# Where the MLP turns the next block's tokens: from between the two second layers of a step to the middle of its first layer

## The chip, the cores and the metric

The kernel runs on one core of a Trainium2 chip. The metric is the device time of one execution in microseconds (us). TensorE (PE in the profile) multiplies, ScalarE (ACT), VectorE (DVE) and GpSimd (POOL) do elementwise work, SyncE (SP) issues transfers. PEld is TensorE's loading of weights, which overlaps the matmuls.

## The reference

The change lies in the last of three stages (an attention, a mixture of experts, an MLP):

```python
def _moe2_ref(x, w_in, w_out, a, b):          # x: 1792 x 768, w_in: 768 x 2048, w_out: 2048 x 768
    h = x @ w_in                              # first layer
    P = a[0] + a[1] * h + a[2] * h**2 + a[3] * h**3
    Q = 1.0 + np.abs(b[0]) * np.abs(h) + np.abs(b[1]) * h**2
    g = P / (Q + 1e-06)                       # the rational function
    return (g @ w_out).astype(np.float32)     # second layer
```

## The kernel before

The MLP starts near 600 us of the span. Its 1,792 tokens go in five blocks (`BLOCKS`): four of three tiles of 128 tokens and one of two. A block has 16 steps, one for each 128 of the 2,048 hidden features, so there are 80 steps, numbered n; f is the step's place in its block. Operands are split into a high and a low part, so every product is three matmuls.

The order on every engine is the order in which `blocks` writes the instructions; nothing reorders them. A step n issues:

- `first(n)` (L1348 to L1350): 18 matmuls, 6 pieces of the depth by 3, into one of the two PSUM banks of the ring `ph` (the tiles `p_l1`; the trace calls both `p_l`).
- `wout_high` (L1326, ScalarE) and, further down, `wout_low` (L1334, VectorE or GpSimd): the split of a row of w_out that is used two steps later. In the first block VectorE has the low part in even steps and GpSimd in odd ones.
- `win_load(n + 3)` (L1314): a transfer that GpSimd issues.
- `rational(n)`, first part: five ScalarE instructions (L1360 to L1364), of which the first four read the bank of `first(n)`; three on GpSimd (L1365 to L1367); the reciprocal on VectorE (L1368), which waits for the second GpSimd one (L1366).
- `second(0, n - 4)` (L1383 to L1385): nine matmuls (six in the last block). 
- In the steps f = 4, 6, ..., 14 of the blocks 0 to 3 a turn (`x2_pose`): three transposes on TensorE (L1306; two for the last block's tokens) of one sixth of the next block's tokens into a bank, the high part copied out by ScalarE (`pose(0)`, L804), the low part taken by VectorE (`pose(1)`, L806: bank minus high part).
- `rational(n - 1)`, third part: ScalarE's cast to gh (L1373), VectorE's gl (L1374). `rational(n)`, second part: VectorE's product t (L1370), which needs the reciprocal and gh's source.
- `second(1, n - 16)`: nine more matmuls, from the second block on. In the first block a step has 27 matmuls, later 36.

`turn` hands out the tiles of a ring in rotation. Before, a step with a turn takes two banks of `ph`: `first(n)` the one, the transposes the other, and `first(n + 1)` again the one, so that `first(n + 2)` gets the bank of the transposes.

So VectorE's order over a step with a turn is: reciprocal of n, gl of n - 1, product of n, `pose(1)`, `wout_low`. ScalarE's is: `wout_high`, five of `rational(n)`, `pose(0)`, gh of n - 1.

Of the kernel before, what the change touches and what calls it, by code (L numbers as in the profile page):

```python
# [40 lines left out]
class K:  # L41
# [1255 lines left out]
        with self.nc.allow_non_contiguous_dma("one column"):  # L1297
            self.nc.sync.dma_start(out=self.order, in_=self.x2d[1][:N, 384].rearrange("(t p) -> p t", p=128))

    def x2_pose(self, bi, kc, bank="ph"):  # L1300

        nc = self.nc
        nt = self.BLOCKS[bi][1]
        pt = self.turn(bank)[:, : 128 * nt]
        for t in range(nt):
            nc.tensor.transpose(pt[:, 128 * t : 128 * t + 128], self.xr[t // 2][:, t % 2, 128 * kc : 128 * kc + 128], self.ident)  # L1306
        h, l = (x[kc][:, : 128 * nt] for x in self.x2[bi % 2])
        return lambda part: self.split(h, l, pt, parts=(part,))
# [95 lines left out]
    def blocks(self):  # L1404
        NF, L, NB = self.NF, self.LAG, len(self.BLOCKS)
        rat, out = self.started, []
        total = NB * NF
        for n in range(total + NF):
            b, f = divmod(n, NF)
            second = [n - L, n - NF]  # L1410
            if b < NB:
                if n not in rat:
                    ph = self.first(n)
            for nh in range(2):
                self.wout_high(nh, second[nh] + 2)
            if n:
                self.win_load(n + 3)
            if b < NB:
                if n not in rat:
                    rat[n] = self.rational(ph, n)  # L1420
                    next(rat[n])
            pose = None
            if 0 <= second[0] < total:
                self.second(0, second[0])
            if b + 1 < NB and 4 <= f < 16 and f % 2 == 0:
                pose = self.x2_pose(b + 1, (f - 4) // 2)
                pose(0)
            if n - 1 in rat:
                next(rat[n - 1])
            if b < NB:  # L1430
                next(rat[n])
            if pose:
                pose(1)
            for nh in range(2):
                self.wout_low(nh, second[nh] + 2)
            if out:
                out.pop(0)()
            last = n >= total + NF - 2
            if 0 <= second[1] and not last:
                self.second(1, second[1])  # L1440
            for nh in range(2):
                if second[nh] >= 0 and second[nh] % NF == NF - 1 and not last:
                    bi = second[nh] // NF
                    if bi < NB:
                        out += [self.result(bi, nh, t) for t in range(self.BLOCKS[bi][1])]
            if f == 0 and b + 1 < NB:
                self.x2_load(self.BLOCKS[b + 1])
            if n == 4:
                self.targets()
            if n == NF - 7:  # L1450
                for k in range(3):
                    self.wout_load(1, k)
        for x in out:
            x()

        nt = self.BLOCKS[-1][1]
        for t in range(nt):
            self.second(1, total - 2, [t])
            self.second(1, total - 1, [t])
            self.result(NB - 1, 1, t, t == nt - 1)()  # L1460
# [31 lines left out]
```

## Time and profile before

| | |
|---|---|
| median of 3 runs | 1111.56 us (1111.51 to 1115.95) |
| profiled execution: its own time | 1112.95 us |
| profiled execution: span | 1111.3 us |
| share of the span busy: PE, PEld, DVE, ACT, POOL | 95%, 77%, 62%, 60%, 63% |
| mean granted TensorE clock | 0.981 of full speed |

The shares are means over three stages with different limits, so the argument goes by the MLP's own stretches. A line of the trace in order of time has the start, the duration, the engine, the line of the kernel, the operation with its output and inputs, and in brackets the engine's idle time before it and what ended it. Instructions of one engine overlap a little at their ends: a matmul of 384 columns shows 0.33 us, and the next starts 0.17 us after it.

### The profile page before, as it was taken

The page shows a single profiled execution, that of the slowest core. Times are in us where ns is not written, and L with a number is a line of the kernel's source. Part 1 is how long each engine was busy: PE and PEld are TensorE (multiplying, and loading weights), DVE is VectorE, ACT ScalarE, POOL GpSimd, SP SyncE. Part 2 cuts the span into 40 slices and gives each one's busy share as a digit, 9 for nine tenths or more (in the row PEclk, how much of TensorE's full clock was granted, in tenths as well). Part 3 has the DMA queues.
Part 4 walks back from the last instruction along what each step waited for, and adds up shares of the span by engine and source line. Part 5 has one row for each costly group of instructions (what it writes and reads, how often), then busy time and mean ns, then how long its engine had stood idle before and what let it go on. Part 6 is the DMA issues. An engine that isn't in the chain of part 4 may idle for free. (4 is left out here: it accounts for less than half of the span.)

```text
span 1111.3 us, 17228 instructions
## 1 busy us (share of the span) xinstructions
PE 1055.2 (95%) x5808; PEld 856.9 (77%) x5808; DVE 689.6 (62%) x862; ACT 672.3 (60%) x1052; POOL 701.6 (63%) x738
## 2 busy tenths in 40 slices
PE   6999999988999989998999889999999999999995
PEld 2332333247898989888889788999999999999995
DVE  3457575878558645936273877666666666665661
ACT  5777777762556535744353666666666666576662
POOL 5767676642546443635253777786787788779974
PEclk8999999998999999999999899999999999999999
DMA  7787878763889775968526565766576566557843
GB/s 190 231 260 227 261 224 262 261 224 133 305 308 366 255 273 166 364 226 305 166 73 225 171 211 167 252 195 196 179 247 216 184 219 214 194 191 232 259 153 112
DMA packets 96441, 247.12 MB, mean 222 GB/s; under 512 B 12321, under 2 KB 61377, under 8 KB 96321
## 3 DMA queue, kind: packets, MB, share of 16 engines
q1 hardware_dynamic: 78624, 161.22, 44.1%
q0 software_dynamic: 17248, 82.62, 22.7%
q10 hardware_dynamic: 448, 1.80, 0.4%
q8 instruction: 60, 0.98, 0.4%
q14 instruction: 61, 0.49, 0.1%
HBM read 202.93 MB, written 42.67 MB: 221 GB/s over the span
## 5 line engine op out<-in xcount | busy, mean ns | idle before, releaser
L1368 DVE RECIPROCAL raw<-raw 128x384 f32<-128x384 f32 (+1 forms) x80 | 191.4, 2392 | 160.6 <-POOL raw L1366 160.6
L840 PE MATMUL p_l<-w1h,x 128*128 128x512 f32 x432 | 143.9, 400 | 1.4 <-ACT x L804 1.4
L1365 POOL TENSOR_TENSOR ex<-ex 128x384 f32<-128x384 f32 (+1 forms) x80 | 78.4, 980 | 84.2 <-ACT ex L1362 83.4
L1360 ACT ACTIVATE ex<-p_l 128x384 f32<-128x384 f32 (+1 forms) x80 | 37.6, 470 | 143.3 <-PE p_l L1350 136.4
L861 PE MATMUL p_l<-w2h,hh 128*128 128x384 f32 x288 | 102.7, 357 | 10.1 <-issue 9.2
L863 PE MATMUL p_l<-w2h,hl 128*128 128x384 f32 x288 | 99.6, 346 | 2.2 <-DVE hl L806 2.0
L136 PE MATMUL sc<-qq,kk 64*128 64x448 f32 (+1 forms) x384 | 96.3, 589 | 5.0 <-DMA kk<-in_k 5.0
L862 PE MATMUL p_l<-w2l,hh 128*128 128x384 f32 x288 | 98.9, 344 | 0.0
L840 PEld LDWEIGHTS p_l<-w1h,x 128*128 128x128 f32 x432 | 82.0, 190 | 18.5 <-ACT x L804 2.2
L143 ACT ACTIVATE ex<-sc,icap 128x896 f32<-128x896 f32 x72 | 70.8, 1004 | 31.1 <-PE sc L136 31.1
L806 DVE TENSOR_TENSOR hl<-p_ht,hh 128x512 fp32r<-128x512 f32 x36 | 24.8, 688 | 102.4 <-ACT hh L804 102.4
L840 PE MATMUL p_l<-w1l,x 128*128 128x512 f32 x216 | 85.3, 397 | 0.7 <-POOL w1l L806 0.7
L1366 POOL TENSOR_TENSOR raw<-raw,ex 128x384 f32<-128x384 f32 (+1 forms) x80 | 80.0, 1000 | 9.0 <-ACT raw L1364 1.7
L843 ACT ACTIVATE hr<-p_l 128x512 f32<-128x512 f32 x36 | 21.6, 599 | 104.1 <-PE p_l L840 104.1
L873 POOL DMA_DIRECT2D x2d<-y x36 | 20.5, 570 | 98.2 <-DVE y L866 64.3
L1106 POOL TENSOR_TENSOR ci_hl<-ci_hl,ci_a 128x384 int32<-128x384 int32 x32 | 41.8, 1328 | 60.2 <-DVE ci_a L1103 47.8
L151 ACT ACTIVATE ex<-ex,cap 128x1792 f32<-128x1792 f32 (+1 forms) x48 | 76.9, 1603 | 1.6
L136 PEld LDWEIGHTS sc<-qq,kk 64*128 64x128 f32 (+1 forms) x384 | 29.3, 176 | 58.2 <-ACT ex L143 18.2
L166 PE MATMUL av<-ex,vv 128*64 128x448 f32 x288 | 69.5, 571 | 0.8 <-ACT ex L151 0.8
L1106 POOL TENSOR_TENSOR c_r<-c_r,c_a 128x768 int32<-128x768 int32 x20 | 36.9, 1846 | 47.9 <-ACT c_a L1096 32.5
L861 PEld LDWEIGHTS p_l<-w2h,hh 128*128 128x128 f32 x288 | 55.9, 194 | 11.3 <-issue 9.8
L806 DVE TENSOR_TENSOR w2l<-ex,w2h 128x1536 fp32r<-128x1536 f32 x24 | 64.5, 2714 | 0.0
(326 smaller groups left out, 3306.3 us busy)
## 6 DMA issues: line engine op xcount, KB each, us to landing
w1h<-wi POOLq DMA_DIRECT2D x40, 768.0 KB, 4.6
w1l<-wi POOLq DMA_DIRECT2D x40, 768.0 KB, 5.1
raw<-in_w SPq DMA_DIRECT2D x34, 768.0 KB
ex<-in_w SPq DMA_DIRECT2D x32, 768.0 KB
raw<-wd SPq DMA_DIRECT2D x80, 192.0 KB
ex<-wd SPq DMA_DIRECT2D x80, 192.0 KB
ci_raw<-in_w SPq DMA_DIRECT2D x16, 768.0 KB
wi<-ci_hl SPq DMA_DIRECT2D x16, 768.0 KB
```

Source lines behind the costliest of these rows:

```text
L136: nc.tensor.matmul(o, kk[half[a], 128 * c : min(128 * c + 128, S)], qq[half[a]], start=True, stop=True)
L143: nc.scalar.activation(out=es[n][:, 2 * c : 2 * c + 2], in_=pt[:, :, :S], func=AF.Tanh, scale=self.icap)
L151: nc.scalar.activation(out=e, in_=e, func=AF.Exp, scale=self.cap)
L806: (eng or nc.vector).tensor_tensor(out=lo, in0=src, in1=hi.bitcast(F32), op=ALU.subtract)
L840: nc.tensor.matmul(pt, a[:, kc, :], b, start=kc == 0 and k == 0, stop=kc == 5 and k == 2)
L861: nc.tensor.matmul(pt[:, :384], hh, wh, start=f == 0, stop=False)
L862: nc.tensor.matmul(pt[:, :384], hh, wl, start=False, stop=False)
L863: nc.tensor.matmul(pt[:, :384], hl, wh, start=False, stop=f == 7)
L1106: self.nc.gpsimd.tensor_tensor(out=r.bitcast(I32), in0=r.bitcast(I32), in1=a.bitcast(I32), op=ALU.add)
L1365: nc.gpsimd.tensor_tensor(out=q, in0=q, in1=s, op=ALU.mult)
L1366: nc.gpsimd.tensor_tensor(out=u, in0=u, in1=t, op=ALU.add)
L1368: nc.vector.reciprocal(out=u, in_=u)
```

## The change

The three transposes are issued after the first three of the six depth pieces of `first(n)`, and the two copies right behind `first`'s middle, ahead of everything else in the step. They go into the bank of the ring that `first(n)` doesn't use, and the ring isn't turned for them, so that `first` takes the two banks in strict alternation.

```diff
-    def x2_pose(self, bi, kc, bank="ph"):
+    def x2_pose(self, bi, kc, bank=None):
...
-        pt = self.turn(bank)[:, : 128 * nt]
+        if bank:
+            pt = self.turn(bank)[:, : 128 * nt]
+        else:
+            at, tiles = self.rings["ph"]
+            pt = tiles[(at + 1) % len(tiles)][:, : 128 * nt]
...
                 if n not in rat:
-                    ph = self.first(n)
+                    pose = b + 1 < NB and 4 <= f < 16 and f % 2 == 0
+                    ph = self.first(n, range(3))
+                    if pose:
+                        pose = self.x2_pose(b + 1, (f - 4) // 2)
+                        pose(0)
+                        pose(1)
+                    self.first(n, range(3, 6), ph)
...
-            pose = None
             if 0 <= second[0] < total:
                 self.second(0, second[0])
-            if b + 1 < NB and 4 <= f < 16 and f % 2 == 0:
-                pose = self.x2_pose(b + 1, (f - 4) // 2)
-                pose(0)
             if n - 1 in rat:
                 next(rat[n - 1])
             if b < NB:
                 next(rat[n])
-            if pose:
-                pose(1)
```

## Rows read from the trace of the kernel before

**Rows 1.** Windows: busy time by engine, granted clock (PEclk), middle of the MLP.
```profile
690.00:790.00 100.00, 100.00 (x584) 99.81 (x583) 65.94 (x70) 64.69 (x136) 75.02 (x86) 1.00 0.65 206
```

**Rows 2.** Waits of PE, 600 to 690 us: total, times, longest.
```profile
PE p_l L1348 <- DVE x2l L806: 2.6, 4, 0.6
```

**Rows 3.** Order of time, PE, first block: where first(10), first(11), first(12) start.
```profile
655.16 0.44 PE L1348 MATMUL p_l<-w1h,w1h 128*128 128x384 f32 x1 [0.65 <-DVE x2l L806]
...
660.74 0.45 PE L1348 MATMUL p_l<-w1h,w1l 128*128 128x384 f32 x1 [0.29 <-ACT ex L1363]
...
666.36 0.45 PE L1348 MATMUL p_l<-w1h,w1h 128*128 128x384 f32 x1 [0.64 <-DVE x2l L806]
```

**Rows 4.** Order of time, ACT: first instruction of rational(10) and of rational(11).
```profile
658.60 0.49 ACT L1360 ACTIVATE ex<-p_l 128x384 f32<-128x384 f32 x1 [2.06 <-PE p_l L1350]
...
664.25 0.49 ACT L1360 ACTIVATE ex<-p_l 128x384 f32<-128x384 f32 x1 [1.78 <-PE p_l L1350]
```

**Rows 5.** Order of time, DVE, step 10: reciprocal, product, low part of the turn.
```profile
662.41 2.55 DVE L1368 RECIPROCAL raw<-raw 128x384 f32<-128x384 f32 x1 [2.00 <-POOL raw L1366]
...
665.29 0.54 DVE L1370 TENSOR_TENSOR ex<-ex,raw 128x384 f32<-128x384 f32 x1
665.75 0.55 DVE L806 TENSOR_TENSOR x2l<-p_l,x2h 128x384 fp32r<-128x384 f32 x1
```

**Rows 6.** Order of time, POOL: first of rational(10); win_load behind step 11's work.
```profile
660.21 1.06 POOL L1365 TENSOR_TENSOR ex<-ex 128x384 f32<-128x384 f32 x1 [0.79 <-ACT ex L1362]
...
670.04 0.58 POOL L1314 DMA_DIRECT2D w1l<-wi  x1
```

**Rows 7.** Order of time, PE, start: first(4), second(0, 0) after its wait, first(5).
```profile
616.63 0.45 PE L1348 MATMUL p_l<-w1h,w1h 128*128 128x384 f32 x1 [2.34 <-ACT ex L1363]
...
624.26 0.44 PE L1384 MATMUL p_xt<-wol,gh 128*128 128x384 f32 x1 [2.50 <-DVE wol L1334]
...
627.06 0.67 PE L1348 MATMUL p_l<-w1h,w1l 128*128 128x384 f32 x1
```

**Rows 8.** Order of time, ACT: last read of step 3's bank; rational(5), (6), (16) begin.
```profile
620.05 0.68 ACT L1363 ACTIVATE ex<-p_l,ab 128x384 f32<-128x384 f32 x1
...
631.07 0.49 ACT L1360 ACTIVATE ex<-p_l 128x384 f32<-128x384 f32 x1 [1.75 <-PE p_l L1350]
...
635.71 0.49 ACT L1360 ACTIVATE ex<-p_l 128x384 f32<-128x384 f32 x1 [1.15 <-PE p_l L1350]
...
692.24 0.49 ACT L1360 ACTIVATE ex<-p_l 128x384 f32<-128x384 f32 x1 [1.65 <-PE p_l L1350]
```

**Rows 9.** Order of time, DVE: the products of steps 3, 6 and 39.
```profile
627.01 1.35 DVE L1370 TENSOR_TENSOR ex<-ex,raw 128x384 f32<-128x384 f32 x1
...
642.91 0.55 DVE L1370 TENSOR_TENSOR ex<-ex,raw 128x384 f32<-128x384 f32 x1
...
846.49 1.37 DVE L1370 TENSOR_TENSOR ex<-ex,raw 128x384 f32<-128x384 f32 x1
```

**Rows 10.** Order of time, POOL, beside the products of steps 6 and 39.
```profile
642.98 1.33 POOL L1365 TENSOR_TENSOR ex<-ex 128x384 f32<-128x384 f32 x1 [1.49 <-ACT ex L1362]
...
840.98 0.58 POOL L1314 DMA_DIRECT2D w1h<-wi  x1 [1.77 <-PE p_ht L1385]
...
846.44 1.01 POOL L1365 TENSOR_TENSOR ex<-ex 128x384 f32<-128x384 f32 x1 [0.39 <-ACT ex L1362]
```

**Rows 11.** Order of time, PE: the longest wait of the last block.
```profile
1043.58 0.44 PE L1384 MATMUL p_xt<-wol,gh 128*128 128x384 f32 x1 [2.07 <-DVE wol L1334]
```

**Rows 12.** Windows, columns as in the first group: the stretch soon after that wait.
```profile
1044.80:1048.20 3.40, 3.40 (x14) 3.40 (x13) 3.40 (x5) 1.93 (x6) 3.38 (x5) 0.52 0.86 252
```

**Rows 13.** Order of time, PE, second block: first(19), first(20) and first(21).
```profile
707.64 0.33 PE L1348 MATMUL p_l<-w1h,w1l 128*128 128x384 f32 x1
...
713.88 0.33 PE L1348 MATMUL p_l<-w1h,w1h 128*128 128x384 f32 x1
...
720.48 0.33 PE L1348 MATMUL p_l<-w1h,w1l 128*128 128x384 f32 x1
```

**Rows 14.** Order of time, DVE: the last instruction of step 19.
```profile
718.11 0.55 DVE L1334 TENSOR_TENSOR x<-raw,x 128x384 fp32r<-128x384 f32 x1
```

## The prediction

> **What bounds the kernel now.** I read the windows first. In the MLP's middle TensorE is busy 100.00 of 100 us at the full clock, GpSimd 75, VectorE 66, ScalarE 65 [rows 1]. There, in the blocks 1 to 3, TensorE alone sets the pace, and a change that gives it the same matmuls in another order gains nothing; it can only lose, if it makes TensorE wait. The first block is the exception: a step has only 27 matmuls, and the list of waits puts idle time of TensorE on VectorE's instruction L806, `pose(1)` [rows 2]. In the order of time each pair of steps of that block (one with a turn, one without) shows two waits: `first(11)` waits 0.29 us for ScalarE's reads of the bank, `first(12)` 0.64 us for `pose(1)` [rows 3]. So what the change can win or lose by waits lies in the first block, steps 4 to 16, and what it finds behind `first(16)` is full: a shift there is carried to the end by a TensorE that doesn't rest.
>
> The pace of that block is a loop. I write S(n) for the start of the first ScalarE instruction of `rational(n)`, which follows the last matmul of `first(n)`. From S(10) = 658.60 [rows 4] the steps are: GpSimd's first product at +1.61 [rows 6], the reciprocal at +3.81, VectorE's product at +6.69, `pose(1)` at +7.15, done at +7.70 [rows 5], and `first(12)` starts at +7.76 [rows 3]; its 18 matmuls bring the next S. One turn of the loop is 11.20 us, from 655.16 to 666.36 [rows 3]. TensorE's own work in it is less. A step of 36 matmuls takes 6.24 us (707.64 to 713.88), one with a turn 6.60 (713.88 to 720.48) [rows 13], so a matmul costs 0.173 and a turn 0.36; two steps of 27 and a turn are 9.7 us. The loop, not TensorE, sets 11.20.
>
> **The change, part by part.** *Work removed or added: none.* 24 turns stay, with 24 casts and 24 subtractions. Only places and banks change.
>
> *The bank wait of 0.29 us goes.* `first` now alternates strictly, so it no longer returns to a bank whose reads have just begun. But `first(n + 1)` now takes the bank of the turn in step n, so it waits for `pose(1)` of n, where before `first(n + 2)` did. And VectorE takes instructions in order: `pose(1)` of n stands now behind the reciprocal and the product of n - 1, where before it stood behind those of n. The chain from S(n - 1) over reciprocal, product and `pose(1)` to `first(n + 1)` has the same members as the old one, one step earlier. So the loop is kept: 11.20 us for two steps, five times from S(5) to S(15), with one wait of about 1.3 us in place of the two. The gain that the freed ring promises does not come.
>
> *A new collision in the loop.* The product has both inputs in SBUF and shares something with GpSimd. In step 6 it started 0.07 us before GpSimd's next product and took 0.55; in step 39 GpSimd had started 0.05 us before it, and the same instruction took 1.37 and ended 0.41 after GpSimd's [rows 9, 10]. That is 0.82 us more. Where does it fall now? After S(n - 1), n even, TensorE no longer waits before `first(n)`: S(n) comes 27 matmuls and a turn later. 27 matmuls without a wait are S(6) - S(5) = 635.71 - 631.07 = 4.64 [rows 8]; with the turn's 0.36 it is 5.00. GpSimd's first product of n is ready 1.61 later, at S(n - 1) + 6.61. GpSimd is free then: its last task ahead of it, the transfer's issue, started in step 11 at 670.04, S + 5.79, and lasts 0.58 [rows 4, 6]. VectorE's product of n - 1 starts at +6.69. GpSimd is 0.08 us ahead, which is the case of step 39. So I take 1.37 for the product in the five loops from S(5) to S(15), that is 11.20 + 0.82 = 12.02 us each. The other bound is 0.55 and 11.20; the two known offsets, 0.05 and 0.07 us, leave the margin thin.
>
> The Trainium skill (SBUF — State Buffer, section Who interferes with whom) has a rule that speaks against this change: a VectorE instruction with two SBUF inputs contends with GpSimd's reads, and "Issue order, not op shape, decides who blocks." The rows of steps 6 and 39 agree with it. By it the whole matter is who is first, so a product that is 0.08 us late is held each time, which gives the sum below; with the order reversed it gives the sum of the first rival.
>
> *A longer single wait, and the clock.* In a loop of 12.02 us TensorE rests once, some 2.0 to 2.2 us, where before it rested twice for less. The two longest free gaps of the MLP, 2.34 before `first(4)` [rows 7] and 2.07 in the last block [rows 11], were of that size, and soon after the second the clock was granted at 0.52, the lower level (1.2 GHz), for 3.4 us [rows 12]. A fall costs 0.48 x 3.40 = 1.6 us of matmuls, and here it would hit `first(n + 1)`, which lies on the loop. I take three falls in five loops, 4.9 us; the bounds are none and five (8.2).
>
> *The start.* The transposes of step 4 go into the bank of `first(3)`, whose last read ends at 620.05 + 0.68 = 620.73 [rows 8]. So TensorE, which begins `first(4)` at 616.63, stops in its middle near 618.3 for some 2.4 us. This is covered: at the end of `first(4)` it waited 2.50 us, until 624.26, for VectorE anyway [rows 7]. Uncovered is the next step: `first(5)`, which started at 627.06 [rows 7], now waits for `pose(1)` of step 4, which VectorE gets to when the product of step 3 ends at 627.01 + 1.35 = 628.36 [rows 9]. With 0.55 for it, `first(5)` starts near 628.9, 1.85 us later. Before, it took 4.01 us to S(5); without a spell of low clock it takes 3.5, with a whole one some 5. So S(5) is 1.3 to 3.5 later; I take 2.0.
>
> *From S(5) to S(16).* Before: 692.24 - 631.07 = 61.17 [rows 8]. After: five loops and the 4.64 of a step without a wait: 5 x 12.02 + 4.64 = 64.7, or +3.6.
>
> *The blocks 1 to 3.* Eighteen turns in the middle of an accumulation instead of between two `second`: the same three transposes, so 0 for 0.36; I allow 0.1 us on either side for each, 1.8. `first(21)` now needs `pose(1)` of step 20. VectorE is through with step 19 at 718.11 + 0.55 = 718.66 [rows 14], `pose(1)` ends at 719.2, and `first(21)` starts at 720.48 [rows 13]: 1.3 us to spare, so no wait. What would break that cover is a late GpSimd: the one wait of 1.77 us [rows 10], with a held product's 0.82 behind it, is 1.3 us more than there is. I take 0 for it and keep 1.3 for the range. ScalarE's new order puts `pose(0)` ahead of `wout_high` and of `rational(n)`; it falls into the 1.8 to 2.1 us that ScalarE waits for `first` [rows 4], and `wout_high` has two steps of lead. SP's queue is passed by nothing; GpSimd's gets no new member.
>
> *Sum:* 2.0 + 3.6 + 4.9 = 10.5. The profiled execution took 1112.95 (span 1111.3), which is 1.39 above the median 1111.56. So 1123.4 in its terms, 1122.1 against the median.
>
> **The rivals.**
> 1. *The product isn't held.* If S(n) comes 0.1 us later than I have it, or the product a little sooner, VectorE is first. Then the loops stay at 11.20: 5 x 11.20 + 4.64 = 60.6, 0.5 less than before, and TensorE's wait of some 1.3 us per loop stays under the gaps that went with low clock. Sum: 2.0 - 0.5 = +1.5, 1113.1. For it speaks the margin of 0.08 us; against it that all loops repeat the same offsets. Chance 0.30.
> 2. *Held, but the clock stays.* For it: the gaps are a little shorter than 2.07. Sum: 2.0 + 3.6 = +5.6, 1117.2, right on the line of half a percent. Chance 0.12.
> 3. *It does what a freed ring suggests, faster.* If `pose(1)` were done before TensorE gets to `first(n + 1)`, at S(n - 1) + 6.2 or sooner instead of +7.70, the loop would open and TensorE's own 9.7 us set the pace: 5 x 9.75 + 4.64 = 53.4, 7.8 less than before, and with the start's 2.0 it is -5.8, 1105.8. Against it stands VectorE's order: from 3.81 to 6.3 it is in the reciprocal. Chance 0.06.
> 4. *The turn in the middle costs more in the full blocks,* by a wait in `first` or at `first(n + 1)`: with 0.5 us in each of 18 turns it is +9 on top of the first rival, 1122. Nothing in the rows shows it. Chance 0.07.
>
> **The numbers.** My forecast, held products and falls of the clock, gets 0.45: 1122.1, with a range of its own from 1118 to 1128.5 (one fall and a start of 1.3; five falls, a start of 3.5 and the 1.3 us of a late GpSimd). The range over all cases reaches down to the first rival with its low start and a little of the turns' allowance, 1111, and up to 1127. Half a percent, 5.6 us, is about what a measurement of this kernel can tell from no change. Faster by that: the third rival, 0.06. Slower: the forecast, half of the second rival, the fourth: 0.45 + 0.06 + 0.07 = 0.58. Within: 0.36.
>
> **What the profile after would show.** Right: in the first block one wait before every odd `first`, on L806, of some 2 us, and none on L1363; the product L1370 of odd steps at 1.37 us, just behind a start of GpSimd's L1365; PEclk below 1 between 630 and 700 us; S(16) later by about 10 us; 690 to 990 as full as before. Wrong: products of 0.55 with waits of 1.3 (first rival), or no waits at all (third). My prediction fails altogether if VectorE's order there is not that of the text, or if a turn takes TensorE longer inside `first` than between two layers.

## The result, and the profile after

The changed kernel takes 1125.45 us (median of 4 runs, 1123.58 to 1126.89) against 1112.72 us before (4 runs, 1111.51 to 1115.95): a ratio of 1.0123, 95% interval 1.0102 to 1.0144. The profiled execution has a span of 1123.9 us (before 1111.3) and its own time of 1125.47 (before 1112.95).

Line numbers of the MLP are 4 higher after, so L1360 is L1364, L1366 is L1370 and L1370 is L1374; L1306 is L1310 and L1348 is L1352. S(n) is, as in the prediction, the start of the first ScalarE instruction (L1360, after: L1364) of step n. S(5) and S(16) after, which answer to [rows 8]:

```profile
631.31 0.49 ACT L1364 ACTIVATE ex<-p_l 128x384 f32<-128x384 f32 x1 [4.62 <-PE p_l L1354]
...
704.03 0.49 ACT L1364 ACTIVATE ex<-p_l 128x384 f32<-128x384 f32 x1 [0.71 <-PE p_l L1354]
```

Cut at S, the two executions differ so:

| from, to | before | after | difference |
|---|---|---|---|
| start to S(0): the stages ahead, same code | 604.96 | 602.23 | -2.73 |
| S(0) to S(5) | 26.11 | 29.08 | +2.97 |
| S(5) to S(16) | 61.17 | 72.72 | +11.55 |
| S(16) to S(17) | 6.24 | 6.24 | 0 |
| S(17) to S(64): later blocks | 298.03 | 300.07 | +2.04 |
| S(64) to S(79): last block | 77.29 | 75.67 | -1.62 |

The loss is in the first block. The list of TensorE's waits, 600 to 705 us, answers to [rows 2]:

```profile
PE p_l L1352 <- DVE x2l L806: 8.2, 4, 2.1
PE p_l L1352 <- DVE w1l L806: 5.1, 2, 3.0
PE p_l L1352 <- ACT ex L1367: 2.3, 1, 2.3
PE p_l L1310 <- ACT ex L1367: 2.3, 1, 2.3
PE p_xt L1388 <- DVE wol L1338: 1.2, 1, 1.2
```

`pose(1)` (L806; its output is w1l or x2l, the two halves of one ring) now ends six waits with 13.3 us in all. The waits for ScalarE's reads before odd steps are gone. In the order of time, TensorE, the wait comes once in two steps and is 2.06 us instead of 0.29 and 0.64 [rows 3]; here before `first(9)` and `first(11)`:

```profile
653.47 0.49 PE L1352 MATMUL p_l<-w1h,w1l 128*128 128x384 f32 x1 [2.06 <-DVE x2l L806]
...
667.11 0.47 PE L1352 MATMUL p_l<-w1h,w1l 128*128 128x384 f32 x1 [2.06 <-DVE x2l L806]
```

Just ahead of the second of them, VectorE and, below, GpSimd:

```profile
664.82 0.50 DVE L1378 TENSOR_TENSOR gl<-ex,gh 128x384 fp32r<-128x384 f32 x1
665.24 1.35 DVE L1374 TENSOR_TENSOR ex<-ex,raw 128x384 f32<-128x384 f32 x1
666.50 0.55 DVE L806 TENSOR_TENSOR x2l<-p_l,x2h 128x384 fp32r<-128x384 f32 x1
```

```profile
665.13 1.04 POOL L1369 TENSOR_TENSOR ex<-ex 128x384 f32<-128x384 f32 x1 [0.35 <-ACT ex L1366]
```

GpSimd starts 0.11 us before the product of step 9, and the product takes 1.35 us, not 0.55 as in [rows 5]; `pose(1)` of step 10 stands behind it. Then the clock falls. Windows of the changed kernel (busy time by engine, granted clock behind POOL's, DMA share, GB/s):

```profile
667.60:671.00 3.40, 3.40 (x12) 3.40 (x12) 3.40 (x4) 0.00 (x0) 1.33 (x2) 0.53 1.00 322
...
650.00:660.00 10.00, 7.94 (x37) 7.62 (x36) 7.31 (x8) 4.95 (x11) 4.83 (x6) 0.83 0.62 197
...
710.00:800.00 90.00, 90.00 (x527) 89.81 (x526) 59.52 (x64) 59.01 (x122) 68.13 (x78) 1.00 0.66 208
800.00:900.00 100.00, 98.25 (x573) 97.74 (x572) 64.02 (x69) 66.15 (x137) 76.16 (x88) 1.00 0.65 208
```

Behind the wait that ended at 667.11 the granted clock is 0.53 for 3.4 us, the lower level. Such a stretch follows each of the five waits of 2.06 us between S(5) and S(16), and two steps take 13.60 to 13.64 us instead of 11.20. From 710 us on TensorE is full again, as in [rows 1], but for 1.75 us between 800 and 900. That is the one late GpSimd, here TensorE and then GpSimd:

```profile
861.80 0.44 PE L1352 MATMUL p_l<-w1h,w1l 128*128 128x384 f32 x1 [1.75 <-DVE x2l L806]
```

```profile
853.12 0.57 POOL L1318 DMA_DIRECT2D w1h<-wi  x1 [1.77 <-issue]
```

The same GpSimd wait stood in [rows 10] without cost. The start, TensorE again; it answers to [rows 7]:

```profile
618.04 0.55 PE L1310 MATMUL p_l<-ident,raw 128*128 128x128 f32 x3 [2.29 <-ACT ex L1367]
...
621.53 0.44 PE L1388 MATMUL p_xt<-wol,gh 128*128 128x384 f32 x1 [1.18 <-DVE wol L1338]
...
626.25 0.56 PE L1352 MATMUL p_l<-w1h,w1l 128*128 128x384 f32 x1 [3.04 <-DVE w1l L806]
```

The transposes of step 4 wait 2.29 us in the middle of `first(4)`; the wait behind it shrinks from 2.50 to 1.18. Uncovered is the 3.04 us before `first(5)`. Its first eleven matmuls then start 0.32 us apart instead of 0.17, at the low clock, as in the stretch behind 667.11.

In the last block the wait that answers to [rows 11] came again, 2.00 us, but the stretch behind it kept the full clock where [rows 12] shows 0.52. This stage is not the change's doing: all twelve kernels of this document have that wait, 2.00 to 2.07 us, and the low clock follows it in six of them. Its row and its window:

```profile
1057.34 0.44 PE L1388 MATMUL p_xt<-wol,gh 128*128 128x384 f32 x1 [2.00 <-DVE wol L1338]
```

```profile
1058.50:1061.90 3.40, 3.40 (x27) 3.40 (x26) 3.40 (x5) 1.99 (x5) 3.38 (x5) 1.00 0.89 266
```

### The profile page after: what moved, and what is told of

Same layout as the page of the kernel before. It is cut to its first block, busy times and chain, and to the rows that moved or that the text cites. A ratio compares the mean times of both kernels' runs of the same rounds, so it can differ in the third digit from the quotient of the medians.

```text
span 1123.9 us, 17224 instructions
## 1 busy us (share of the span) xinstructions
PE 1056.0 (94%) x5808; PEld 861.1 (77%) x5808; DVE 693.2 (62%) x862; ACT 674.9 (60%) x1052; POOL 700.6 (62%) x738
## 5 line engine op out<-in xcount | busy, mean ns | idle before, releaser
L1364 ACT ACTIVATE ex<-p_l 128x384 f32<-128x384 f32 (+1 forms) x80 | 37.6, 471 | 119.3 <-PE p_l L1354 118.4
L806 DVE TENSOR_TENSOR hl<-p_ht,hh 128x512 fp32r<-128x512 f32 x36 | 24.8, 689 | 102.2 <-ACT hh L804 102.0
L1370 POOL TENSOR_TENSOR raw<-raw,ex 128x384 f32<-128x384 f32 (+1 forms) x80 | 79.4, 993 | 9.4 <-ACT raw L1368 1.5
L1352 PE MATMUL p_l<-w1h,w1l 128*128 128x384 f32 (+1 forms) x176 | 60.8, 345 | 15.1 <-DVE x2l L806 10.0
```

What stands on the lines that cost most here:

```text
L1370: nc.gpsimd.tensor_tensor(out=u, in0=u, in1=t, op=ALU.add)
```

## The experiments

Every kernel is timed against the kernel before on the same chip. The stages ahead of S(0) are the same code everywhere, yet S(0) lies between 600.1 and 608.1 us in the profiled executions, so the table of stages at the end of this section says more about each edit than the times do. An edit that adds lines shifts the numbers again: the product is L1378 in e1_order and e5_order6, and L1374 in the other experiments.

**The collision, first try.** The changed kernel, with GpSimd's two instructions exchanged in even steps of the first block:

```diff
+        early = n < self.NF and n % 2 == 0
+        if early:
+            nc.gpsimd.tensor_tensor(out=u, in0=u, in1=t, op=ALU.add)
         nc.gpsimd.tensor_tensor(out=q, in0=q, in1=s, op=ALU.mult)
-        nc.gpsimd.tensor_tensor(out=u, in0=u, in1=t, op=ALU.add)
+        if not early:
+            nc.gpsimd.tensor_tensor(out=u, in0=u, in1=t, op=ALU.add)
```

> The changed kernel with one edit: in the even steps of the first block GpSimd computes u + t (which the reciprocal waits for) ahead of q * s, so that GpSimd's first instruction of an even step starts some 7.7 us after S of the step before instead of 6.6, behind VectorE's product. Theory (held product, then falls of the clock): the product of odd steps goes from 1.35 to 0.55 us, TensorE's wait before odd first from 2.06 to about 1.2, no fall of the clock in the five loops, a loop 11.2 instead of 13.6 us, so 5 x 2.4 = 12 us less: about 1113. Rival (a turn inside first costs more by itself, or the new wait is as long whatever GpSimd does): 1120 or more. Second rival (the clock falls with waits of 1.2 us too): about 1121.

Measured: 1120.77 us, ratio 1.0079 (1.0053 to 1.0105). The five loops are as expected, 11.25 to 11.27 us, products of 0.54, no fall of the clock in them; S(5) to S(16) is 60.94. But the edit also touched steps 0 to 4 and did harm there: S(0) to S(5) is 31.36, against 29.08 in the changed kernel, so that the total missed the theory's 1113 and lies where the rival put it. VectorE's gl (L1382) of step 1 took 4.38 us, and TensorE then waited 3.72 us for the `wout_low` behind it:

```profile
622.43 4.38 DVE L1382 TENSOR_TENSOR gl<-ex,gh 128x384 fp32r<-128x384 f32 x1
```

**The collision alone.** The same from step 6 on:

```diff
-        early = n < self.NF and n % 2 == 0
+        early = 6 <= n < self.NF and n % 2 == 0
```

> The edit of e1_order, but from step 6 on, so that the start stays as in the changed kernel. Theory (held product, then falls of the clock): S(5) - S(0) 29.1 us as in the changed kernel, S(16) - S(5) 60.9 as in e1_order instead of 72.7, so 11.8 us less than the changed kernel: about 1113.6. Rival (e1_order's remaining 9 us over the kernel before are a cost of the changed place itself): 1119 or more.

Measured: 1116.3 us, ratio 1.0041 (1.0023 to 1.0058). The stages are as expected to 0.1 us: 29.08, then 60.96 against 72.72. TensorE before `first(11)`, the product ahead of it, GpSimd's first instruction of step 10, and a window over the waits of the five loops:

```profile
667.47 0.44 PE L1352 MATMUL p_l<-w1h,w1l 128*128 128x384 f32 x1 [1.26 <-DVE x2l L806]
```

```profile
666.41 0.54 DVE L1378 TENSOR_TENSOR ex<-ex,raw 128x384 f32<-128x384 f32 x1
```

```profile
667.46 1.00 POOL L1371 TENSOR_TENSOR raw<-raw,ex 128x384 f32<-128x384 f32 x1 [1.51 <-ACT raw L1368]
```

```profile
644.00:692.00 48.00, 42.04 (x239) 40.64 (x240) 33.01 (x35) 32.37 (x66) 33.94 (x38) 1.00 0.59 196
```

So the held product and what follows from it are 11.8 us of the change's loss. The total lies between theory and rival. The stages agree with it: in the profiled pair S(0) to S(17) is 2.8 us longer than in the kernel before, S(17) to S(64) 3.6 longer and the last block 1.6 shorter, 4.8 in all, and the medians differ by 4.9. Of the 3.6, 1.6 are new: the wait of 1.74 us in the third block, which the changed kernel has too, is followed here by the low clock. TensorE and the window:

```profile
855.90 0.44 PE L1352 MATMUL p_l<-w1h,w1l 128*128 128x384 f32 x1 [1.74 <-DVE x2l L806]
```

```profile
857.50:860.90 3.40, 3.40 (x13) 3.40 (x12) 2.15 (x4) 0.05 (x1) 0.24 (x1) 0.51 0.80 262
```

The theory's 1113.6 came from the changed kernel's total, which lies 12.7 us above the kernel before, where its stages from S(0) to S(79) add up to 14.9.

**The clock alone.** The changed kernel with nine spare matmuls ahead of `first` in the steps 5, 7, ..., 15:

```diff
+                    if n < NF and n % 2 and n > 4:
+                        for k in range(9):
+                            o = slice(128 * (k % 6), 128 * (k % 6) + 128)
+                            nc.tensor.matmul(self.acc[1][1][:, :384], self.win[n][:, o], self.x2[0][0][k % 6][:, :384], start=True, stop=True)
                     ph = self.first(n, range(3))
```

> The changed kernel with nine extra matmuls of 384 columns at the head of the steps 5, 7, ..., 15, into a bank of the second layer that is not in use yet; their result is not used. They fill 1.6 us of TensorE's wait and change nothing else. Theory: the product stays held at 1.35 us, the wait shrinks to about 0.5 us, the clock no longer falls, a loop is 12.0 instead of 13.6: 5 x 1.6 = 8 us less, about 1117. Rival (the low clock is no part of the loop's length): 1125, or more by the extra work, up to 5 x 1.6 = 8 us more, 1133.

Measured: 1118.73 us, ratio 1.0065 (1.0039 to 1.0091). More work, less time: 12.06 to 12.08 us per loop, S(5) to S(16) 64.98. The product is still held, the wait is 0.52, the clock full:

```profile
658.94 1.37 DVE L1374 TENSOR_TENSOR ex<-ex,raw 128x384 f32<-128x384 f32 x1
```

```profile
660.84 0.44 PE L1352 MATMUL p_l<-w1h,w1l 128*128 128x384 f32 x1 [0.52 <-DVE x2l L806]
```

```profile
636.00:688.00 52.00, 49.36 (x283) 47.77 (x282) 37.75 (x36) 32.10 (x64) 36.49 (x40) 1.00 0.54 178
```

So the falls of the clock are 7.7 us of the 11.8, and the held product by itself 4.

**The place alone,** the ring turned as before:

```diff
-                        pose = self.x2_pose(b + 1, (f - 4) // 2)
+                        pose = self.x2_pose(b + 1, (f - 4) // 2, "ph")
```

> The changed kernel, but with the ring turned for the transposes as before: the early place alone, without the strict alternation. Theory (what costs is that first of the next step waits for the low part of the turn): first of the odd steps waits for ScalarE's reads again, some 0.6 us, and for nothing on VectorE; a loop is some 10.6 us, so S(5) to S(16) about 57.6 us, 3.6 less than in the kernel before: about 1108. Rival (the place inside first is what costs): 1120 or more.

Measured: 1113.56 us, ratio 1.0016 (0.9998 to 1.0033). The rival falls: the place inside `first` is not what costs. But my 1108 was missed too; S(5) to S(16) is 63.41, not 57.6. TensorE's waits on L806 are down to 0.2 us in all, as expected; in their stead ScalarE waits for VectorE. The longest in its list of waits, 625 to 692 us:

```profile
ACT gh L1377 <- DVE ex L1374: 21.5, 12, 4.2
```

Eight of the eleven products between 626 and 692 us are held at 1.36 or 1.37 us here, and gl of every fourth step takes 3.37 to 4.35 us, the longest:

```profile
680.23 4.35 DVE L1378 TENSOR_TENSOR gl<-ex,gh 128x384 fp32r<-128x384 f32 x1
```

VectorE falls behind, and gh, which stands ahead of the next step's five instructions on ScalarE, waits for it. S(0) to S(5) is 24.87 with the ring turned, so the start's loss too comes with the bank and not with the place.

**The other half alone:** the old place, the other bank, no turn of the ring. `blocks` is that of the kernel before, and:

```diff
-        pt = self.turn(bank)[:, : 128 * nt]
+        at, tiles = self.rings["ph"]
+        pt = tiles[(at + 1) % len(tiles)][:, : 128 * nt]
```

> The other half of the change alone: the transposes where the kernel before has them, but into the bank that the step's first doesn't use and without a turn of the ring. Theory (first of the next step waits for the low part of the turn, which VectorE reaches 7.7 us after S): first(n + 1) starts 7.8 us after S(n). In the first block two steps take 15.9 us and more instead of 11.2; in the later blocks, where first(n + 1) starts 3.3 us after S(n) now, each of 18 turns costs 4.5 us, and gaps of 4.5 us bring falls of the clock of 1.6 us: 28 to 38 and 81 to 110 us more, 1220 to 1260. Rival (the bank doesn't matter, the place does): 1112.

Measured: 1275.48 us, a single run; granted clock 0.925. S(5) to S(16) is 96.88, S(17) to S(64) 419.12 against 298.03. It is 15 us above the range that I gave; the list of waits shows the mechanism, 24 waits, one for each turn, 4.75 us in the mean:

```profile
PE p_l L1352 <- DVE w1l L806: 71.2, 16, 6.4
PE p_l L1352 <- DVE x2l L806: 42.8, 8, 6.4
```

So strict alternation is what binds `first` to VectorE, and the early place is what makes that nearly bearable.

**The later blocks alone:** in the first block the turn as before (late, ring turned), the blocks 1 to 3 changed.

```diff
-                        pose = self.x2_pose(b + 1, (f - 4) // 2)
-                        pose(0)
-                        pose(1)
+                        if b:
+                            pose = self.x2_pose(b + 1, (f - 4) // 2)
+                            pose(0)
+                            pose(1)
...
+            late = n < NF and 4 <= f and f % 2 == 0
+            if late:
+                pose = self.x2_pose(1, (f - 4) // 2, "ph")
+                pose(0)
             if n - 1 in rat:
                 next(rat[n - 1])
             if b < NB:
                 next(rat[n])
+            if late:
+                pose(1)
```

> The change in the blocks 1 to 3 alone; the first block as in the kernel before. Theory (the loss lies in the first block, the later ones are TensorE's, with 1.3 us to spare): as the kernel before, at the most 1.8 us more by the one wait in step 40: 1112 to 1114. Rival (each turn inside first costs TensorE something): 18 x 0.2 to 0.5 us more, 1116 to 1121.

Measured: 1112.41 us, ratio 1.0006 (0.9989 to 1.0023). S(17) to S(64) is 300.05, as in the changed kernel, with a single wait of TensorE from 700 to 1000 us:

```profile
PE p_l L1352 <- DVE x2l L806: 1.7, 1, 1.7
```

**The loop taken away:** the changed kernel, first block's turns into idle banks of the second layer.

```diff
-            pt = tiles[(at + 1) % len(tiles)][:, : 128 * nt]
+            pt = (tiles[(at + 1) % len(tiles)] if bi > 1 else self.acc[1][kc % 3])[:, : 128 * nt]
```

> The changed kernel, but in the first block the transposes go into the three banks of the second layer's other half, which are not used until step 16; the later blocks as changed. Theory (the loop over the shared bank sets the pace of the first block): the loop is gone, no wait on L806 in the first block, two steps take TensorE's own 9.7 us, S(5) to S(16) about 53 us against 61.2 before: about 1104. Rival (VectorE's or GpSimd's work sets the pace of the first block by itself): no faster than 1110.

Measured: 1112.46 us, ratio 1.001 (0.9996 to 1.0024). The loop is gone (no wait on L806), but from S(7) to S(13) two steps take 10.7 us, not 9.7: the rival was right that VectorE sets the pace then. It is busy 55.68 of 58 us, since nearly every product and low part of w_out is held by GpSimd. Windows, then the list of waits, 630 to 690:

```profile
630.00:688.00 58.00, 54.63 (x314) 52.88 (x312) 55.68 (x44) 41.60 (x85) 49.30 (x49) 1.00 0.63 194
```

```profile
ACT gh L1377 <- DVE ex L1374: 14.6, 10, 1.7
```

**Loop and collision taken away.** As the last, with the later blocks' ring turned, `early = 6 <= n < self.NF`, and VectorE given all low parts of w_out from step 6 on:

```diff
-            eng = n % 2 if not nh and n < self.NF - self.LAG or ...
+            eng = n % 2 if not nh and n < 4 or ...
...
+        pt = (self.acc[1][kc % 3] if bi == 1 and not bank else self.turn(bank or "ph"))[:, : 128 * nt]
```

> A try at a version faster than both: turns in the middle of first; in the first block into the unused banks of the second layer (no loop over the ring), later ones with the ring turned; from step 6 on in the first block GpSimd computes u + t first, and VectorE has all the low parts of w_out (no GpSimd instruction under VectorE's product). Theory: nothing is held, two steps of the first block take TensorE's 9.7 us, S(16) - S(5) 53.5 to 55 us against 61.2 before and S(17) - S(16) 6.2: about 1105. Rival (VectorE and GpSimd get into each other's way again as in e4_spare_mid): 1110 to 1112.

Measured: 1106.16 us, ratio 0.9947 (0.9924 to 0.9971): faster than both. Two steps take 9.71 or 9.72 us, S(5) to S(16) 53.25. Only S(16) to S(17) is long, 8.71: the product of step 15 took 4.51 us. VectorE and, below, GpSimd:

```profile
686.43 4.51 DVE L1374 TENSOR_TENSOR ex<-ex,raw 128x384 f32<-128x384 f32 x1
```

```profile
686.03 0.57 POOL L1314 DMA_DIRECT2D w1l<-wi  x1
686.62 1.03 POOL L1368 TENSOR_TENSOR ex<-ex 128x384 f32<-128x384 f32 x1
687.59 1.01 POOL L1370 TENSOR_TENSOR raw<-raw,ex 128x384 f32<-128x384 f32 x1
688.56 1.01 POOL L1371 TENSOR_TENSOR ex<-ex 128x384 f32<-128x384 f32 x1
689.53 0.98 POOL L1334 TENSOR_TENSOR x<-ex,x 128x384 fp32r<-128x384 f32 x1
```

**The order kept up to step 19:**

```diff
-        early = 6 <= n < self.NF
+        early = 6 <= n < 20
```

> e8_open with GpSimd's order u + t first kept up to step 19 instead of step 15, so that in step 16 it leaves a space in which VectorE's product of step 15 can start. Theory (that product waited 4.51 us because four GpSimd instructions stood close together): it takes 0.55 to 1.4 us, S(17) - S(16) is 6.2 instead of 8.7 us: 2.5 us less than e8_open, about 1104. Rival (the wait comes from the fuller steps 14 to 16 in any order): as e8_open, 1106.

Measured: 1102.8 us, ratio 0.9922 (0.9907 to 0.9936), the lowest ratio, though its interval overlaps that of e8_open. S(16) to S(17) is 6.81; the product of step 15 takes 2.62 us, more than I gave it:

```profile
685.21 2.62 DVE L1374 TENSOR_TENSOR ex<-ex,raw 128x384 f32<-128x384 f32 x1
```

TensorE is full in the first block:

```profile
627.00:688.00 61.00, 61.00 (x358) 60.84 (x358) 52.24 (x53) 45.82 (x93) 46.36 (x52) 1.00 0.66 207
```

**The same with the turn in the old place:** the kernel before, with the order and the low parts of the last, and:

```diff
-        pt = self.turn(bank)[:, : 128 * nt]
+        pt = (self.acc[1][kc % 3] if bank == "ph" and bi == 1 else self.turn(bank))[:, : 128 * nt]
```

> The kernel before, with the turns where it has them (between the second layers), and only the other edits of e9_open20: in the first block the unused banks, GpSimd's order and VectorE's low parts. Theory (bank and order decide, the place of the turn does nothing): S(16) - S(5) 53.3 us and the same time as e9_open20, about 1104. Rival (the place in the middle of first is worth something once the loop is gone): 2 us or more above e9_open20.

Measured: 1104.88 us, ratio 0.9938 (0.992 to 0.9957). Its interval overlaps that of the last, and S(0) to S(17) is 86.20 against 85.81 us. The medians differ by the rival's 2 us, but the stages of the profiled pair place only 0.4 of them where the edit acts, and the other 1.6 in the last block, where the low clock follows the wait in this kernel and not in the last one; the times don't tell the two apart.

| kernel | S(0) to S(5) | S(5) to S(16) | S(16) to S(17) | S(17) to S(64) |
|---|---|---|---|---|
| before | 26.11 | 61.17 | 6.24 | 298.03 |
| changed | 29.08 | 72.72 | 6.24 | 300.07 |
| e1_order | 31.36 | 60.94 | 6.24 | 299.93 |
| e5_order6 | 29.08 | 60.96 | 6.24 | 301.65 |
| e2_fill | 28.02 | 64.98 | 6.24 | 301.52 |
| e3_mid_turn | 24.87 | 63.41 | 8.47 | 297.43 |
| e6_old_noturn | 33.41 | 96.88 | 6.24 | 419.12 |
| e7_later_blocks | 26.68 | 61.16 | 6.24 | 300.05 |
| e4_spare_mid | 25.74 | 58.12 | 8.47 | 299.47 |
| e8_open | 25.74 | 53.25 | 8.71 | 297.43 |
| e9_open20 | 25.76 | 53.24 | 6.81 | 298.23 |
| e10_open_old | 26.08 | 53.25 | 6.87 | 298.23 |

## Why the prediction was right

It was right in mechanism and direction: "slower" and 1122.1 us were forecast, 10.5 above the kernel before; 1125.45 was measured, 12.7 above it and within the range. The sizes of the terms were less good than that.

- *The loop is kept, one step earlier.* Shown. With the collision taken out (e5_order6) two steps take 11.26 us, against 11.20 forecast, and the single wait is 1.26 against some 1.3.
- *The held product.* Shown by its row, and by the exchange of two GpSimd instructions. S(n) to S(n + 1) from odd to even came out at 4.97 where I had 5.00, so GpSimd was ahead by 0.11 us, not 0.08. The Trainium skill's rule (SBUF — State Buffer, section Who interferes with whom) says that issue order decides who blocks, and the loops agree with it: the product that started 0.11 us behind GpSimd took 1.35 us. The last section has rows that don't fit it.
- *The clock.* Right in kind, too small in size: I took three falls, there were five of five, in each loop alike. That is 2 x 1.6 us, and S(5) to S(16) grew by 11.55, not 8.5. The spare matmuls (e2_fill) show the falls by themselves. The prediction called 2.34 and 2.07 the two longest gaps; the 2.50 of [rows 7] is longer.
- *The start.* 2.97 instead of 2.0, inside the bounds. The stall in the middle of `first(4)` was covered as described, and `first(5)` started 1.92 us later, counted from S(0), for 1.85 forecast. What was too small is the clock again: from there to S(5) it took 5.06 us, what the prediction had for a whole spell of low clock, and not the 4.2 that are in its 2.0.
- *The later blocks.* The turn costs the same in either place: S(19) to S(20) is 6.59 after, S(20) to S(21) 6.59 before. The term that I set to nothing, the wait after a late GpSimd, came: 1.75 us, and 2.04 in the stage; e7_later_blocks shows it alone. Its bound, 1.3, was too low.
- In the profiled pair these make +16.6, where 10.5 was forecast: as much as the upper bounds of the forecast's terms, which give 1128.2 (the text has 1128.5), beyond the stated range that ends at 1127. 2.7 us that the same code ahead of S(0) took less, and 1.6 that the last block's clock gave back, bring it to 12.2; the difference of the spans is 12.6. That the total came so near the forecast is luck to that extent.

The first rival's sum, +1.5, left out the late GpSimd; e5_order6, which is that rival, has +2.97 at the start, -0.2 in the loops and the later blocks' loss. The third rival, an open loop of 9.7 us, was built in e8_open, though not by this change.

What stays open: why GpSimd waits 1.77 us at one issue in the third block, and so whether that wait can be had away. It stands in the traces of all twelve kernels, right behind the issue of the ninth indirect transfer of results, and no run changes anything about it.

## What to carry to other kernels

Before a consumer is given another buffer, follow who frees it: a ring that needs no turn saves nothing if its next writer now waits for the last instruction of a longer queue. In a loop closed over several in-order engines, write down each start as an offset from one event; here an offset of 0.11 us between VectorE and GpSimd decided 0.8 us in each loop, and the wait of 2.06 us that came of it cost 1.6 us more through the clock. Opening the loop alone (e4_spare_mid) won nothing, and moving the collision alone (e5_order6) left the kernel slower than before; the gain came with both together. What GpSimd's order and VectorE's low parts each did for it was not run apart.

## What the runs showed of the hardware that was not expected

A VectorE instruction with two SBUF inputs that has to wait for GpSimd mostly waits for one instruction of it, even where the next stands ready. In the changed kernel the product of step 3 took 1.34 us and came in between L1370 and L1371, which show no pause between them; VectorE and, below, GpSimd:

```profile
624.38 1.34 DVE L1374 TENSOR_TENSOR ex<-ex,raw 128x384 f32<-128x384 f32 x1
```

```profile
624.20 1.10 POOL L1370 TENSOR_TENSOR raw<-raw,ex 128x384 f32<-128x384 f32 x1 [0.16 <-ACT raw L1368]
625.27 1.31 POOL L1371 TENSOR_TENSOR ex<-ex 128x384 f32<-128x384 f32 x1
```

But it can wait through several: four in a row, 4.51 us for 0.55 of work, in e8_open and 4.38 in e1_order, and two in e9_open20 (2.62). There it got its turn when GpSimd came to a transfer's issue or paused for 0.08 us. In these rows VectorE's instruction had started 0.08 to 0.19 us ahead of the first GpSimd instruction that it waited for, while GpSimd was ending the issue of a transfer (in e8_open 686.43 against 686.62), so by the starts that the trace shows it was first and was held all the same. Why some wait for one and some for several stays open.

The fall of the clock came after all five waits of 2.06 us in the loops, and after none of the five of 1.25 or 1.26 us in e5_order6. Between these it went both ways: after the third block's wait of 1.74 or 1.75 us it came in two of the six kernels that have it (e5_order6 and e2_fill), after the last block's of 2.00 to 2.07 us in six of twelve.
